# Sliding-window attention into an MLP: block 11's input transposed on TensorE and ScalarE instead of by DMA

## The chip, the cores and the metric

The kernel runs on one core of a Trainium2 chip. The metric is the device time of one execution in microseconds (us). A core has five engines that work at once, each in its own order: TensorE (PE: matmuls, with the weight loads PEld beside them), VectorE (DVE), ScalarE (ACT), GpSimd (POOL) and SyncE (SP). POOL and SP mostly issue DMA transfers here. Engines wait for each other with semaphores.

## The reference, cut to what matters

```python
# q, k, v: batch 8, heads 8, tokens 576, head size 64
scores = q @ k.T / 8 - slope[head] * |query - key|   # only 0 <= query - key < 128
x  = softmax(scores) @ v                             # heads side by side: (8, 576, 512)
xn = (x - mean(x)) / sqrt(var(x) + 1e-6) * g_ln
out = x + relu(xn @ w_ch1) @ w_ch2                   # 512 -> 2048 -> 512
```

## The kernel before, in words

**Blocks and groups.** The 8 x 576 tokens are cut into 36 blocks of 128: four pairs of batches, nine blocks each (eight full ones, and a ninth, `T`, that holds the 64 last tokens of both batches). Block number n is `p * 9 + blk`. `GROUPS = [2] * 4 + [4] * 7` puts blocks 0 to 7 into four groups of two and the rest into seven groups of four, so group 3 holds blocks 6 and 7, and group 4 holds blocks 8 to 11. `home[n]` gives the group of a block and its place in it.

**Attention of a block.** `attend` makes scores on TensorE (L407), ScalarE takes the exponential (L415), VectorE multiplies by the decay and mask (`masks`, L426). `values_at_once` multiplies by v on TensorE (L489); VectorE takes the reciprocal of the row sums (L497) and scales (L498), which gives x of the block. `centre` subtracts the row mean (L540), which gives `xc`, in fp16. `square` sums the squares of `xc` on ScalarE (L571); `inv_std` makes the inverse standard deviation of a whole group on VectorE (L585 to L603). That factor is multiplied in only at the end (L949, L831), so the MLP runs on `xc` itself.

**The transposed x.** The first layer needs x with its features on the partitions: tile `xT` of a group, four chunks of 128 features by up to 512 tokens. Blocks 0 to 7 (`BY_DMA = 8`) get it by `turn_x`: four TensorE transposes (matmuls with an identity, L560) into one PSUM tile `ps_tx`, and one copy to SBUF (L561) by VectorE or ScalarE. From block 8 on, `centre` issues one DMA transpose per block from SP (L550). SP's queue also carries the stores of the output (L970, L965) and, from block 18 on, the DMA transposes of q and k (`turn_natural`, L327); it is in order.

**The MLP of a group.** `mlp1` runs the first layer: for each of 16 chunks of 128 hidden units four matmuls with the whole group as the moving side (L718), and a ReLU by ScalarE (L734) or VectorE (L726). For groups of two, `mlp2` runs the second layer: for each block 16 matmuls (L748), then `finish` (L949) and `store`. Groups of four go through `mlp2_seven`, a scheme with seven products of half size instead of eight (L810, L831) with sums prepared on VectorE (L768).

**The order.** TensorE, ScalarE, VectorE and SP run in the order in which the program is written (`tc.manual_schedule`). The attention is a list of `steps`, four for each block from block 8 on; the MLP functions are generators that yield after every four first-layer matmuls or every two second-layer matmuls. `weave_at(units, *places)` runs the MLP unit by unit and, behind the units whose numbers it is given, the next step of the list. The second layer of group 3 carries all four steps of block 11, and the first layer of group 4 follows it:

```python
weave_at(mlp2(3), 0, 2, 3, 6, 9, 11, sums=4)
for g in range(4, len(GROUPS)):
    one, two = LEAD[g - 4]
    weave_at(mlp1(g, (6, 13) if one else ()), *one, seven=g)
```

The four steps of a block are: values, centring and the first scores of a later block; the second scores; the first masks and `square`; the second masks. Of block 11 they stand behind units 3, 6, 9 and 11 of the sixteen of `mlp2(3)`. The steps of block 12 begin behind unit 2 of `mlp1(4)`, that is, after twelve first-layer matmuls.

**PSUM.** One pool, `ps_mm`, of four banks serves the transposes (`ps_tx`, `ps_tr`), the accumulators of both layers (`ps_m1`, `ps_m2`, both shown as `ps_m` in the profile) and the seven products (`ps_s`); the scores have two tiles of their own, `ps_sc`.

**Loads.** POOL issues the loads of q, k and v in one list, six or seven blocks ahead; a load waits until its buffer is free.

Of the kernel before, what the change touches and what calls it, by code (L numbers as in the profile page):

```python
# [30 lines left out]
FIRST_GROUPS, FIRST = 2, 4  # L31

BY_DMA = SEEN = 8

# [36 lines left out]
def kernel(  # L73
# [10 lines left out]
    nc = tc.nc  # L84
# [148 lines left out]
    def by_dma(p, blk):  # L233
        return p * NSLOT + blk >= TURN_BY_DMA
# [10 lines left out]
    order = [(p, blk) for p in range(NPAIR) for blk in range(NSLOT)]  # L245
# [183 lines left out]
    def attends(p, blk):  # L429

        low, high, every = [0, 1], [2, 3], [0, 1, 2, 3]
        if blk == T:
            return [(p, T, [6, 7], m_ends, "probs", hps) for hps in (low, high)]
        if blk < 2:
            return [(p, blk, [blk], m_full[:, :, P:], "own", every)]
        return [(p, blk, [blk - 2, blk], m_full, "probs", hps) for hps in (low, high)]
# [5 lines left out]
    def tail_attend(p):  # L442
        return (p, T, [T], m_tail, "own", [0, 1, 2, 3])
# [66 lines left out]
    centred = {}  # L510

    def centre(p, blk):

        total = sums.pop((p, blk))
        mean = small.tile([P, 1], FP32, tag="mean", name="mean")
        if p * NSLOT + blk < BY_DMA:
            nc.vector.tensor_scalar(
                out=mean,
                in0=total[:, 0:1],
                scalar1=total[:, 1:2],  # L520
                scalar2=1.0 / DM,
                op0=ALU.add,
                op1=ALU.mult,
            )
        else:
            nc.vector.tensor_scalar(
                out=mean, in0=total[:, 0:1], scalar1=1.0 / DM, scalar2=None, op0=ALU.mult
            )
        xc = xc_pool.tile([P, DM], FP16, tag="xc", name="xc")
        if p == 0 and blk < FIRST:  # L530
            nc.vector.scalar_tensor_tensor(
                out=xc,
                in0=xs[p, blk],
                scalar=mean,
                in1=g_row,
                op0=ALU.subtract,
                op1=ALU.mult,
            )
        else:
            nc.vector.tensor_scalar(  # L540
                out=xc, in0=xs[p, blk], scalar1=mean, scalar2=None, op0=ALU.subtract
            )
        n = p * NSLOT + blk
        g, at = home[n]
        if at == 0:
            turned_x[g] = group_pool.tile([P, NKB, 4 * P], FP16, tag="xT", name="xT")
        if n < BY_DMA or g >= SEVEN:
            centred[p, blk] = xc
        if n >= BY_DMA:
            nc.sync.dma_start_transpose(  # L550
                out=turned_x[g][:, :, at * P : (at + 1) * P], in_=xc
            )

    def turn_x(g, at, p, blk, copy):

        xT = turned_x[g]
        xc = centred.pop((p, blk))
        ps = ps_mm.tile([P, NKB, P], FP16, tag="mm", name="ps_tx")
        for kb in range(NKB):
            nc.tensor.transpose(ps[:, kb, :], xc[:, kb * P : (kb + 1) * P], iden)  # L560
        copy(out=xT[:, :, at * P : (at + 1) * P], in_=ps)  # L561
# [47 lines left out]
    members, home = [], {}  # L609
    for g, size in enumerate(GROUPS):  # L610
        n = sum(GROUPS[:g])
# [5 lines left out]
    def turn_step(n, *how):  # L617
        p, blk = order[n]
        return [(turn, p, blk // 2) + how]
# [4 lines left out]
    def values_steps(n):  # L624
        p, blk = order[n]
        ahead = place[min(n + AHEAD + (n > TURN_BY_DMA - 10), count - 1)]
        return [
            [(load_until, ahead), (masks, p, blk), (values, p, blk, 0)],
            [(values, p, blk, 1), (centre, p, blk)],
        ]  # L630

    def x_step(n, copy=nc.vector.tensor_copy):
        return [(turn_x,) + home[n] + order[n] + (copy,)] if n < BY_DMA else []

    def variance_of(n):

# [5 lines left out]
    def warm_step(n):  # L642
        return [[(warm, n)]]


    steps = warm_step(11) + [[(turn_first,)]] + warm_step(3)
    steps += [scores_step(0), scores_step(1) + masks_of(0) + masks_of(1)] + warm_step(6)
    steps += values_steps(0)
    steps += [turn_step(2, True, (nc.scalar.copy, nc.scalar.copy))]
    steps += values_steps(1) + warm_step(4)  # L650
    steps += [x_step(0, nc.scalar.copy)] + warm_step(2) + [scores_step(2)]
    steps += [masks_of(2, 1) + x_step(1) + scores_step(3), values_steps(2)[0]]
    steps += [masks_of(2)]
    first = len(steps)

    steps += [values_steps(2)[1] + masks_of(3)]
    steps += [x_step(2, nc.scalar.copy), *values_steps(3), x_step(3, nc.scalar.copy)]

    steps += [variance_of(0) + variance_of(1), variance_of(2) + variance_of(3)]
# [14 lines left out]
    for n in range(8, count):  # L674
        ahead = place[min(n + AHEAD + (n > TURN_BY_DMA - 10), count - 1)]
        todo = []
        if n + 1 < count and order[n + 1][1] == T:
            todo.append(tail_attend(order[n][0]))
        if n + 2 < count:
            todo += attends(*order[n + 2])  # L680
        step = [(load_until, ahead), (masks,) + order[n]]
        step += [(values_at_once,) + order[n], (centre,) + order[n]]
        step += [(attend, *args, 1) for args in todo[:1]]
        second = [(attend, *args, 1) for args in todo[1:]]
        if n + 3 < count and order[n + 3][1] % 2 == 0 and not by_dma(*order[n + 3]):
            second += turn_step(n + 3)
        third = [(masks, *args[:2], 1) for args in todo[:1]] + [(square, n)]
        for tag, m in (("q", n + 4), ("k", n + 5)):
            if m < count and order[m][1] % 2 == 0 and by_dma(*order[m]):
                p, blk = order[m]  # L690
                third.append((turn_natural, tag, p, blk // 2))
        steps += [step, second, third, [(masks, *args[:2], 1) for args in todo[1:]]]
    TWICE = [4, 6, 8, 9, 11, 13, 15, 15], [3, 7, 11, 15, 19, 23, 27, 27]
    LEAD = [([2, 4, 5, 6, 7, 8, 9, 10, 12, 13, 15, 15], TWICE[1])]
    LEAD += 4 * [TWICE] + [(TWICE[0], [7, 11, 15, 19]), ([], [])]
# [352 lines left out]
```

## Time and profile before

| | |
|---|---|
| time before, median of 3 runs | 316.02 us (313.88 to 316.44) |
| the profiled execution, its own time | 316.07 us |
| its span | 314.3 us |
| TensorE busy | 302.9 us, 96% |
| VectorE busy | 233.9 us, 74% |
| ScalarE busy | 184.4 us, 59% |
| POOL busy | 107.9 us, 34% |
| mean granted TensorE clock | 0.994 of full speed |
| first layer, L718 | 576 matmuls, 119.5 us |
| DMA transposes of x, L550 | 28, median 4.4 us from issue to landing |

The span runs from the first to the last instruction of the profiled execution; what the execution's own time has beyond it lies around it. Times in the profile's rows are microseconds from the start of the span. A row of a timeline gives start, duration, engine, line, operation, output and inputs, shapes and count; in square brackets stands the idle time of the engine just before, and what ended it. A matmul's duration includes its way through the array, so matmuls in a row overlap, and the distance of their starts is shorter than the duration of one. The granted clock is 1.00 at full speed. The chain is the work that ended last, followed back from the last instruction.

### The profile page before, as it was taken

Reading aid. Unit: us, or ns where it says so; the run is one execution under the profiler, and the core shown is the slowest. Engines: PE = TensorE matmul, PEld = TensorE weight load, DVE = VectorE, ACT = ScalarE, POOL = GpSimd, SP = SyncE. Lnnn points to the kernel's source line nnn. Section 1 sums busy time; section 2 is a strip of 40 time slices with the busy share of each in tenths; the row PEclk is TensorE's granted clock in tenths of the full one; section 3 lists DMA queues with packets and bytes.
Section 4 is the critical chain, followed back from the end, with each engine's and each line's share of the span. In section 5 each row is a group of like instructions: output and inputs, shape, how many; then the busy total and the mean of one; then the engine's idle time right before and its main releaser. Section 6 shows DMA issues by size and latency. Waiting matters only on the chain.

```text
span 314.3 us, 9387 instructions
## 1 busy us (share of the span) xinstructions
PE 302.9 (96%) x3886; PEld 200.8 (64%) x3886; DVE 233.9 (74%) x629; ACT 184.4 (59%) x330; POOL 107.9 (34%) x148
## 2 busy tenths in 40 slices
PE   8889999998988999999999999999999999999994
PEld 3468655856733568755864686468656865785583
DVE  2689887697993889767976887688769876964563
ACT  6588766767944983467357735753676268405600
POOL 8923758769341634725251645120000000000000
PEclk9999999999997999999999999999999999999999
DMA  9999999999992999999999999993562143025004
GB/s 105 176 206 198 189 146 173 199 146 151 131 117 53 95 105 125 138 197 106 134 126 166 101 141 138 165 135 59 114 108 50 37 94 79 17 19 134 0 19 117
DMA packets 140316, 36.99 MB, mean 118 GB/s; under 512 B 131185, under 2 KB 135921, under 8 KB 140274
## 3 DMA queue, kind: packets, MB, share of 16 engines
q0 software_dynamic: 98560, 18.36, 85.2%
q1 hardware_dynamic: 41234, 17.52, 32.9%
q8 instruction: 30, 0.49, 0.7%
q10 hardware_dynamic: 480, 0.52, 0.5%
q14 instruction: 12, 0.10, 0.1%
HBM read 36.90 MB, written 9.44 MB: 147 GB/s over the span
## 4 chain that ended last, share of the span: by engine, by line
PE 83%; DVE 6%; DMA 5%; ACT 2%; POOL 2%; issue 1%; POOLq 0%
PE ps_m L718 39%; PE ps_s L810 24%; PE ps_sc L407 5%; PE ps_m L748 5%; PE ps_q L889 4%; PE ps_sc L489 4%; DMA k<-in_k_dram 2%; DMA xT<-xc 2%; DMA out_dram<-o 1%; ACT probs L415 1%; PE ps_pv L460 1%; POOL q L204 1%; DVE w L768 1%; DVE k L314 1%; DVE st L565 1%
## 5 line engine op out<-in xcount | busy, mean ns | idle before, releaser
L718 PE MATMUL ps_m<-xT,w1g 128*128 128x512 f16 (+1 forms) x576 | 119.5, 359 | 2.7 <-DMA xT<-xc 2.4
L734 ACT ACTIVATE ht_all<-ps_m 128x512 f16<-128x512 f32 (+1 forms) x159 | 81.9, 519 | 42.8 <-PE ps_m L718 40.6
L718 PEld LDWEIGHTS <-w1g 128*128 128x128 f16 x576 | 54.3, 98 | 54.1 <-issue 5.9
L415 ACT ACTIVATE probs<-ps_sc 128x1024 f16<-128x1024 f32 x56 | 56.6, 1029 | 48.0 <-PE ps_sc L407 48.0
L239 POOL DMA_DIRECT2D vx<-in_v_dram x40 | 34.5, 867 | 33.4 <-PE ps_sc L489 24.8
L810 PE MATMUL ps_s<-w,s 128*128 128x256 f16 x384 | 43.8, 273 | 0.0
L810 PEld LDWEIGHTS <-s 128*128 128x128 f16 x384 | 36.7, 98 | 4.7
L426 DVE TENSOR_TENSOR probs<-probs,m 128x1024 f16<-128x1024 f16 x56 | 36.9, 683 | 1.7 <-ACT probs L415 1.7
L810 PE MATMUL ps_s<-w,ht_all 128*128 128x256 f16 x288 | 34.3, 273 | 0.0
L768 DVE TENSOR_TENSOR s<-ht_all 128x1024 f16<-128x1024 f16 (+2 forms) x35 | 20.4, 582 | 18.3 <-ACT ht_all L734 17.7
L228 POOL DMA_DIRECT2D q<-in_q_dram x32 | 21.9, 703 | 30.2 <-DMA q<-q 23.5
L748 PE MATMUL ps_m<-w,ht_all 128*128 128x512 f16 x128 | 31.0, 380 | 0.0
L810 PEld LDWEIGHTS <-ht_all 128*128 128x128 f16 x288 | 27.4, 98 | 5.0
L831 DVE SCALAR_TENSOR_TENSOR o<-ps_s,rstd,x 128x256 f32<-128x256 f32 x48 | 21.0, 479 | 11.1 <-PE ps_s L810 11.1
L407 PE MATMUL ps_sc<-q,k 64*64 64x128 f16 (+1 forms) x1088 | 24.0, 209 | 0.9 <-ACT probs L415 0.8
L407 PEld LDWEIGHTS <-k 64*64 64x64 f16 x1088 | 15.9, 106 | 12.8 <-issue 10.3
L571 ACT ACTIVATE junk<-xc 128x512 f16<-128x512 f16 x28 | 17.6, 627 | 4.9 <-DVE xc L540 4.8
L498 DVE SCALAR_TENSOR_TENSOR x<-ps_sc,rec 128x512 f16<-128x512 f32 x28 | 19.4, 692 | 1.0
L831 DVE SCALAR_TENSOR_TENSOR o<-ps_s,rstd,o 128x256 f32<-128x256 f32 x36 | 15.7, 479 | 4.5 <-PE ps_s L810 4.4
L748 PEld LDWEIGHTS <-ht_all 128*128 128x128 f16 x128 | 11.2, 98 | 11.2
L225 POOL DMA_DIRECT2D k<-in_k_dram x16 | 14.4, 916 | 10.9 <-DMA k<-k 10.9
L415 ACT ACTIVATE own<-ps_sc 128x1024 f16<-128x1024 f32 x12 | 12.1, 1032 | 9.2 <-PE ps_sc L407 9.2
(88 smaller groups left out, 343.4 us busy)
## 6 DMA issues: line engine op xcount, KB each, us to landing
out_dram<-o SPq DMA_DIRECT2D x66, 128.0 KB, 3.5
k<-in_k_dram POOLq DMA_DIRECT2D x32, 128.0 KB, 6.0
vx<-in_v_dram POOLq DMA_DIRECT2D x32, 128.0 KB, 6.6
w<-in_moe_w_ch_dram POOLq DMA_DIRECT2D x8, 512.0 KB, 10.5
q<-in_q_dram POOLq DMA_DIRECT2D x40, 64.0 KB, 4.2
q<-in_q_dram POOLq DMA_DIRECT2D x16, 128.0 KB, 7.2
k<-in_k_dram POOLq DMA_DIRECT2D x8, 64.0 KB, 4.8
vx<-in_v_dram POOLq DMA_DIRECT2D x8, 64.0 KB, 4.7
```

What stands on the lines that cost most here:

```text
L228: nc.gpsimd.dma_start(out=t[half, b], in_=tokens.rearrange("h (c r) d -> r c h d", r=2)[r],)
L239: nc.gpsimd.dma_start(out=vx[p0 : p0 + n, :, 0:D], in_=v[b, :, t0 : t0 + n, :].rearrange("h p d -> p h d"),)
L407: nc.tensor.matmul(in_halves(ps[cols, j, n, t, :])[:, r, queries], kt[rows, hp, cols], in_halves(qt[rows, b, hp])[:, r, queries], start=Tr ...
L415: nc.scalar.activation(out=dst.rearrange("p (n j) q -> p j n q", j=2), in_=ps.rearrange("p j n t q -> p j n (t q)"), func=AF.Exp, scale=in ...
L426: nc.vector.tensor_tensor(out=dst, in0=dst, in1=mask, op=ALU.mult)
L498: nc.vector.scalar_tensor_tensor(out=x.rearrange("p (h d) -> p h d", h=H), in0=ps[:, :, 0:D], scalar=1.0, in1=rec.unsqueeze(2).broadcast_t ...
L718: nc.tensor.matmul(ps[:, 0:cols], w[:, kb, fb * P : (fb + 1) * P], xT[:, kb, 0:cols], start=(kb == 0), stop=(kb == NKB - 1),)
L734: nc.scalar.activation(out=ht[:, fb, :], in_=ps[:, 0:cols], func=AF.Relu)
L748: nc.tensor.matmul(sums[at], ht[:, fb, at * P : (at + 1) * P], w2[:, fb, :], start=(fb == 0), stop=(fb == NFB - 1),)
L768: nc.vector.tensor_tensor(out=out, in0=a, in1=b, op=op)
L810: nc.tensor.matmul(ps[:, pair, :], lhs[:, fb, at : at + P], rhs[:, fb, :], start=(first and pair == 0 and fb == 0), stop=(fb == half - 1), ...
L831: nc.vector.scalar_tensor_tensor(out=outs[at][:, cols], in0=ps[:, pair], scalar=rstd[:, n : n + 1], in1=(xs[p, blk] if fresh else outs[at] ...
```

## The change

Block 11 is taken out of the DMA path: `centre` issues no DMA transpose for it, and `turn_x` does its four transposes on TensorE and the copy on ScalarE. These stand in block 11's fourth step, behind unit 11 of `mlp2(3)`. The second masks of the block's step list move from the fourth step to the third, and `square` of block 11 from the third to the fourth, behind the copy. `turn_x` no longer takes `xc` out of the dictionary, since `square` reads it afterwards. All other blocks are handled as before.

```diff
+IN_HASTE = 11
 ...
-        if n >= BY_DMA:
+        if n >= BY_DMA and n != IN_HASTE:
             nc.sync.dma_start_transpose(
                 out=turned_x[g][:, :, at * P : (at + 1) * P], in_=xc
             )
 ...
     def turn_x(g, at, p, blk, copy):
 
         xT = turned_x[g]
-        xc = centred.pop((p, blk))
+        xc = centred[p, blk]
 ...
     def x_step(n, copy=nc.vector.tensor_copy):
-        return [(turn_x,) + home[n] + order[n] + (copy,)] if n < BY_DMA else []
+        return [(turn_x,) + home[n] + order[n] + (copy,)] if n < BY_DMA or n == IN_HASTE else []
 ...
-        steps += [step, second, third, [(masks, *args[:2], 1) for args in todo[1:]]]
+        fourth = [(masks, *args[:2], 1) for args in todo[1:]]
+        if n == IN_HASTE:
+            third, fourth = third[:1] + fourth, x_step(n, nc.scalar.copy) + third[1:]
+        steps += [step, second, third, fourth]
```

In the built program, VectorE's and POOL's instructions are the same and in the same order as before. SP has one DMA transpose less. TensorE has four weight loads and four transposes more, behind the eighth of the sixteen second-layer matmuls of block 7. ScalarE has the copy more, ahead of `square` of block 11.

## The prediction

> **What bounds the kernel now.** I read the page first: shares, slices, chain.
>
> ```profile
> span 314.3 us, 9387 instructions
> PE 302.9 (96%) x3886; PEld 200.8 (64%) x3886; DVE 233.9 (74%) x629; ACT 184.4 (59%) x330; POOL 107.9 (34%) x148
> ...
> PEclk9999999999997999999999999999999999999999
> ...
> PE 83%; DVE 6%; DMA 5%; ACT 2%; POOL 2%; issue 1%; POOLq 0%
> ```
>
> TensorE is busy for 302.9 of 314.3 us and makes 83% of the chain, so an edit counts by what it does to TensorE's stream. One of the 40 slices shows a granted clock below 9: the thirteenth, 94.3 to 102.1 us. TensorE's own waits come next, with total, times and longest:
>
> ```profile
> PE ps_m L718 <- DMA xT<-xc: 2.4, 1, 2.4
> ...
> PE ps_sc L407 <- ACT probs L415: 0.8, 3, 0.5
> ```
>
> The longest is a single wait of 2.4 us: a first-layer matmul (L718) waits for an x transposed by DMA. The chain in order of time shows which:
>
> ```profile
> 88.74 0.06 DVE xc L540
> ...
> 89.44 5.77 DMA xT<-xc
> ...
> 95.45 4.44 PE ps_m L718 x12
> ```
>
> At 88.74 VectorE centres block 11, the last member of group 4; its transpose is issued at 89.44 and takes 5.77 us; only then can group 4's first layer begin. The windows around it give busy time (PE, PEld, DVE, ACT, POOL), then granted clock, DMA share and GB/s:
>
> ```profile
> 84.00:88.00 4.00, 4.00 (x124) 2.54 (x113) 3.97 (x9) 3.54 (x8) 3.21 (x5) 1.00 1.36 70
> 88.00:93.00 5.00, 5.00 (x38) 2.05 (x36) 4.93 (x10) 2.06 (x4) 2.16 (x3) 1.00 1.73 115
> 93.00:95.45 2.45, 0.04 (x1) 0.03 (x1) 2.17 (x11) 0.00 (x0) 0.00 (x0) 1.00 1.69 186
> 95.45:97.00 1.55, 1.55 (x5) 0.60 (x6) 0.04 (x1) 0.00 (x0) 0.00 (x0) 0.58 0.45 106
> 97.00:99.00 2.00, 2.00 (x6) 0.66 (x5) 0.00 (x0) 0.75 (x2) 0.00 (x0) 0.50 0.03 8
> 99.00:101.00 2.00, 2.00 (x38) 1.31 (x37) 0.55 (x2) 1.31 (x3) 0.34 (x1) 0.97 0.00 0
> ```
>
> After the stall the clock is 0.58, then 0.50, and is back at about 99 us. So the late transpose is paid twice: as idle time, and as slow matmuls.
>
> **The change, part by part.** *Removed: the wait.* TensorE's rows on both sides, and the same twelve matmuls a little later:
>
> ```profile
> 88.98 4.06 PE L748 MATMUL ps_m<-w,ht_all 128*128 128x512 f16 x18
> 95.45 4.44 PE L718 MATMUL ps_m<-xT,w1g 128*128 128x512 f16 x12 [2.42 <-DMA xT<-xc]
> 99.72 0.65 PE L489 MATMUL ps_sc<-vx,probs 128*128 128x65 f16 x16
> ...
> 103.30 2.96 PE L718 MATMUL ps_m<-xT,w1g 128*128 128x512 f16 x12
> 106.09 0.65 PE L489 MATMUL ps_sc<-vx,probs 128*128 128x65 f16 x16
> ```
>
> The idle time is 2.42 us; it goes if x is ready in time (below). Term: -2.42.
>
> *Removed: the slow clock.* Twelve equal matmuls take 4.44 us after the stall and 2.96 us at 103.30. Term: 2.96 - 4.44 = -1.48. Counted to the next group's start, it is (99.72 - 95.45) - (106.09 - 103.30) = 4.27 - 2.79 = 1.48, the same. Its bounds are 0, if the clock falls here for another reason, and 1.48. The Trainium skill (TensorE: Matmul & The Clock Gate, Part 1: The HAM clock gate) has the clock halve after an idle window of about 3.4 us, longer than this stall. By that rule the stall would not explain the fall and this term would be 0; the trace, with 0.58 straight after 2.42 us, speaks for the stall.
>
> *Added: four transposes on TensorE and a copy on ScalarE.* The kernel does the same for blocks 0 to 7:
>
> ```profile
> 26.77 0.38 PE ps_tx L560 x4
> L560 PE MATMUL ps_tx<-iden,xc x32: 219/219/230, 15.5 to 62.2; 128*128 128x128 f16 x32
> L561 ACT COPY xT<-ps_tx x3: 579/586/628, 16.4 to 27.2; 128x512 f16<-128x512 f16 x3
> ```
>
> In the chain four transposes take 0.38 us. Unpipelined they would be 4 x 0.219 = 0.88. I take 0.38, since the stream around them is as dense here; the bounds are 0.38 and 0.88. Term: +0.38. The Trainium skill (the same page, Part 4: PE-mode transpose) puts a transpose at about 275 ns in a kernel, 390 alone, and says that transposes do not count as busy for the gate. By its 275 ns the estimate would be 1.1 us and the sum 313.3. The row with 0.38 for four decides against that.
>
> *Is the input there?* For the time at which TensorE gets there, the group of the second layer (count, busy, mean ns):
>
> ```profile
> L748 PE MATMUL ps_m<-w,ht_all 128*128 128x512 f16 x128 | 31.0, 380 | 0.0
> ```
>
> In the built order the transposes stand after unit 11 of the second layer of group 3: behind ten of the 18 matmuls at 88.98, ahead of the last eight. The last of 18 lasts 0.38 us from its start, so a slot is (4.06 - 0.38) / 17 = 0.216 us. So TensorE reaches them at 88.98 + 10 x 0.216 = 91.1. Block 11's xc:
>
> ```profile
> 88.74 0.67 DVE L540 TENSOR_SCALAR xc<-x,mean 128x512 f16<-128x512 f16 x1
> ...
> 93.08 0.75 DVE L949 SCALAR_TENSOR_TENSOR o<-ps_m,rstd,x 128x512 f32<-128x512 f32 x1
> ...
> 95.32 0.17 DVE L603 SCALAR_TENSOR_TENSOR rstd<-hh,rstd 128x4 f32<-128x4 f32 x1
> 100.42 0.21 DVE L497 RECIPROCAL rec<-ps_sc 128x8 f32<-128x8 f32 x1 [4.93 <-PE ps_sc L489]
> ```
>
> It is done at 89.41, 1.7 us early. VectorE's order does not change.
>
> *Is the copy out of the way?* ScalarE's rows:
>
> ```profile
> 89.11 1.02 ACT L415 ACTIVATE probs<-ps_sc 128x1024 f16<-128x1024 f32 x1 [0.68 <-PE ps_sc L407]
> 90.03 0.62 ACT L571 ACTIVATE junk<-xc 128x512 f16<-128x512 f16 x1
> ...
> 97.14 0.60 ACT L734 ACTIVATE ht_all<-ps_m 128x512 f16<-128x512 f32 x1 [6.41 <-PE ps_m L718]
> ```
>
> The transposes end at 91.1 + 0.38 = 91.5, with up to 0.22 for the last to come through; the copy runs from 91.7 to 92.3. Group 4's first matmul is due after the eight remaining slots, at 91.5 + 8 x 0.216 = 93.2. So those eight hide the copy with 0.9 us to spare; with that cover gone it would cost 0.22 + 0.59 = 0.8. Behind the copy in ScalarE's queue stands block 11's square (L571), which moves from 90.03 to 92.3 and ends near 93.1. Its reader is the inverse deviation of group 4 on VectorE, behind the output sum that now starts at 93.5 and ends at 94.2. So it costs nothing, in ScalarE's gap of 6.41 us. PSUM: the new tile takes one of four shared banks; in the built order the next first-layer tiles wait for banks freed by then, and none of the first three for block 7's sum.
>
> *Removed from SP: one DMA transpose.* The store behind it waits for its own data anyway (SP, POOL, and the landings of xT):
>
> ```profile
> 84.35 1.19 SPq L550 DMA_TRANSPOSE xT<-xc  x1
> 89.44 1.19 SPq L550 DMA_TRANSPOSE xT<-xc  x1
> 90.72 1.18 SPq L970 DMA_DIRECT2D out_dram<-o  x2
> 100.66 0.88 POOL L239 DMA_DIRECT2D vx<-in_v_dram  x1 [10.49 <-PE ps_sc L489]
> DMA to landing us min/median/max: 2.8/5.4/6.0
> ```
>
> The store's sum L949 of block 6 ends at about 90.7, so SP gains nothing: 0. Group 4 still waits for three DMA transposes; the last of them, block 10's at 84.35, is in by 90.4 even with the longest landing of any x from 60 to 140 us (6.0).
>
> *What is late next.* TensorE reaches block 12's values about 3.5 us sooner, at 96.2. VectorE by then has the output sum and the inverse deviation behind it: that ended at 95.32 + 0.17 = 95.49, 1.7 after the sum (93.08 + 0.75 = 93.83), so 94.2 + 1.7 = 95.9 now, in time for the reciprocal (L497), due near 96.9 (0.7 behind the values, as before). POOL's next load waits for TensorE (10.49 us) and moves with it, into DMA engines that are nearly idle (share 0.03 at 97). TensorE's later stretches, and its only other late wait, both from 100 us on:
>
> ```profile
> PE ps_sc L407 <- ACT probs L415: 0.3, 2, 0.2
> ...
> 100.00:140.00 40.00, 39.64 (x572) 26.16 (x569) 31.44 (x81) 26.25 (x43) 20.13 (x26) 1.00 1.43 125
> 140.00:200.00 60.00, 60.00 (x699) 40.35 (x696) 47.83 (x126) 35.91 (x59) 25.07 (x33) 1.00 1.64 135
> 200.00:260.00 60.00, 60.00 (x697) 40.64 (x700) 47.03 (x122) 34.52 (x57) 2.27 (x3) 1.00 0.71 89
> ```
>
> It is full to 260 us, and its one wait there follows its own scores. I find nothing that keeps its absolute time, so the gain should last to the end: 0 given back.
>
> *Sum*, against the profiled execution's 316.07 us (span 314.3 and 1.77 around it): 316.07 - 2.42 - 1.48 + 0.38 = 312.55. That execution is 0.05 above the median of 316.02. I say 312.5.
>
> **The rivals.**
>
> *The clock falls anyway* (chance 0.09): the gate closes on something else near 95 us, or closes at another place once the pace changes. For it: one shown run took 313.88, 2.2 below the profiled one, so something of that size varies between runs. Against it: the clock is 1.00 before the stall and 0.58 right after. Time: 316.07 - 2.42 + 0.38 = 314.03. The rule of the Trainium skill on the 3.4 us window (TensorE: Matmul & The Clock Gate, Part 1), weighed above, would give this same time.
>
> *The copy becomes the wait* (0.09): TensorE stands at group 4's first matmul until ScalarE has written xT. For it: ScalarE is in order and its exponentials of 1.02 us stand just ahead. Against it: 0.9 us of margin, and 0.62 us of ScalarE work (the square) leaves the queue's head. Cover gone entirely and unpipelined transposes: 312.55 + 0.8 + 0.5 = 313.9; half of that is 313.2.
>
> *The change doesn't take the wait away* (0.03): group 4 also needs the DMA transposes of blocks 8 to 10; if the DMA engines, not the late issue, set the date, TensorE waits on for them. Time: 316.07 + 0.38 = 316.45. Against it: 90.4 at the latest, as above.
>
> *TensorE takes over VectorE's lateness: slower* (0.05). Now the whole in-order stream stands at the transposes until xc is there, with eight second-layer matmuls behind them, which used to run meanwhile. VectorE is busy 3.97 of 4 and 4.93 of 5 us here, so nothing of a delay would be caught up. The price is the slip less 1.7, plus 1.48 if the clock halves again. With that, the break-even is 2.42 + 1.48 - 0.38 - 1.48 = 2.04 us of stall, a slip of 3.7 us. A slip of 5 gives a stall of 3.3, and 312.55 + 3.3 + 1.48 = 317.3. Against it: nothing is put ahead of xc on VectorE.
>
> **How the numbers follow.** The forecast has 0.74: 312.5, with its own range 312.2 to 313.1 (transposes at 0.88 above; below, a dead time of 95.45 - 88.98 - 18 x 0.216 = 2.6 us, if slots rather than ends are counted). The whole range, 311.3 to 314.4, takes in the first two rivals, and below a part of the 2.6 us spread of the runs shown (313.88 to 316.44), whose cause I can't see. About 1% is what a measurement of this kernel can tell; faster by more is below 312.9. That has most of the forecast's 0.74: 0.68 for faster. Same: the rest of it, both middle rivals and the third, 0.28. Slower by over 1%: 0.04 of the last rival's 0.05.
>
> **What would show it.** Right: no wait of L718 for DMA near 93; granted clock 1.00 throughout 93 to 101; four L560 transposes near 91 in about 0.4 us; the copy (L561) on ScalarE done before group 4's first matmul; twelve first-layer matmuls in about 2.9 us; block 12's values at about 96 instead of 99.72; later stages all earlier by the same 3.5 us. Wrong: a stall at the transposes or at the first L718; a slice with a lower clock elsewhere; or a later wait of TensorE above 0.5 us that is not there now, which would be the gain given back.

## The result, and the profile after

| | before | changed |
|---|---|---|
| median of 11 runs | 313.93 us (313.16 to 316.44) | 312.28 us (311.69 to 312.97) |
| profiled execution, its own time | 316.07 us | 312.28 us |
| span | 314.3 us | 310.5 us |
| its mean granted clock | 0.994 | 1.000 |

The ratio is 0.9931, with a 95% interval of 0.9906 to 0.9956: faster by 0.7%, not by the forecast 1.1%. (The ratio, here and below, is estimated from the runs of both kernels, without a run over 1.5% above the fastest of its kernel; the quotient of the two medians is 0.995.) The time of the changed kernel was forecast to 0.2 us (312.5), in part by luck, as the part on the prediction shows. What was not foreseen is the other side of the ratio: over 11 runs the kernel before is 2.1 us faster than the three runs shown first, and than the profiled one.

The page of the changed kernel: span, TensorE's share, and its granted clock in the 40 slices; then what is left of the waits of the first layer (L723 here, L718 before).

```profile
span 310.5 us, 9392 instructions
...
PE 301.1 (97%) x3890; PEld 200.3 (65%) x3890; DVE 234.2 (75%) x629; ACT 185.1 (60%) x331; POOL 108.1 (35%) x148
...
PEclk9999999999999999999999999999999999999999
```

```profile
PE ps_m L723 <- DMA w<-in_moe_w_ch_dram: 0.4, 1, 0.4
PE ps_m L723 <- ACT k L316: 0.3, 1, 0.3
```

The wait for `xT` is gone, and so is the slice with the low clock. The timeline around the place, three engines together:

```profile
89.13 0.67 DVE L542 TENSOR_SCALAR xc<-x,mean 128x512 f16<-128x512 f16 x1
...
89.37 2.33 PE L753 MATMUL ps_m<-w,ht_all 128*128 128x512 f16 x10
...
91.54 0.39 PE L562 MATMUL ps_tx<-iden,xc 128*128 128x128 f16 x4
...
91.76 1.89 PE L753 MATMUL ps_m<-w,ht_all 128*128 128x512 f16 x8
91.96 0.59 ACT L563 COPY xT<-ps_tx 128x512 f16<-128x512 f16 x1 [1.44 <-PE ps_tx L562]
...
92.98 0.19 ACT L573 ACTIVATION_READ_ACCUMULATOR junk<-xc 128x1 f32 x1
...
93.49 2.75 PE L723 MATMUL ps_m<-xT,w1g 128*128 128x512 f16 x12
...
95.94 0.16 DVE L605 SCALAR_TENSOR_TENSOR rstd<-hh,rstd 128x4 f32<-128x4 f32 x1
...
96.08 0.65 PE L491 MATMUL ps_sc<-vx,probs 128*128 128x65 f16 x16
...
96.77 0.21 DVE L499 RECIPROCAL rec<-ps_sc 128x8 f32<-128x8 f32 x1 [0.68 <-PE ps_sc L491]
```

xc is done at 89.80, the copy at 92.55, and the first layer, at 93.49, follows the second without a gap. The windows of the stall of before (the last three numbers are granted clock, DMA share, GB/s):

```profile
93.00:95.45 2.45, 2.45 (x14) 1.09 (x12) 2.05 (x8) 0.80 (x4) 0.00 (x0) 1.00 0.42 99
95.45:97.00 1.55, 1.55 (x37) 1.08 (x36) 0.75 (x5) 1.16 (x2) 0.00 (x0) 1.00 0.73 169
97.00:99.00 2.00, 2.00 (x31) 0.87 (x30) 1.21 (x4) 1.65 (x3) 0.88 (x1) 1.00 0.18 11
```

**A measure free of the start.** The first 20 us wait for loads and differ by up to 3 us between executions. So I compare *the stretch*: from the first of the 18 last second-layer matmuls of group 3 to block 12's first v matmul. Before it is 99.72 - 88.98 = 10.74 us, now 96.08 - 89.37 = 6.71: a gain of 4.03. What comes ahead of the stretch is 0.39 longer in this execution, and what follows (314.3 - 99.72 = 214.58, 310.5 - 96.08 = 214.42) is 0.16 shorter: 4.03 - 0.39 + 0.16 = 3.80 of span.

### The profile page after: what moved, and what is told of

Its sections match the earlier page's. It is cut to its first block, busy times and chain, and to the rows that moved or that the text cites. A ratio compares the mean times of both kernels' runs of the same rounds, so it can differ in the third digit from the quotient of the medians.

```text
span 310.5 us, 9392 instructions
## 1 busy us (share of the span) xinstructions
PE 301.1 (97%) x3890; PEld 200.3 (65%) x3890; DVE 234.2 (75%) x629; ACT 185.1 (60%) x331; POOL 108.1 (35%) x148
## 4 chain that ended last, share of the span: by engine, by line
PE 85%; DMA 6%; POOL 3%; DVE 3%; issue 1%; ACT 1%; SPq 0%; POOLq 0%
PE ps_m L723 38%; PE ps_s L815 24%; PE ps_m L753 7%; PE ps_sc L409 5%; DMA w<-in_moe_w_ch_dram 4%; PE ps_sc L491 4%; PE ps_q L894 4%; DMA out_dram<-o 1%; POOL vx L241 1%; POOL k L206 1%; POOL q L206 1%; POOL w L167 1%; ACT probs L417 1%; PE ps_pv L462 1%; DVE st L567 1%
## 5 line engine op out<-in xcount | busy, mean ns | idle before, releaser
L723 PE MATMUL ps_m<-xT,w1g 128*128 128x512 f16 (+1 forms) x576 | 117.8, 356 | 0.3 <-ACT k L316 0.3
L723 PEld LDWEIGHTS <-w1g 128*128 128x128 f16 x576 | 53.9, 98 | 50.2 <-issue 0.8
L409 PEld LDWEIGHTS <-k 64*64 64x64 f16 x1088 | 15.8, 107 | 12.6 <-issue 10.2
```

Source lines behind the costliest of these rows:

```text
L409: nc.tensor.matmul(in_halves(ps[cols, j, n, t, :])[:, r, queries], kt[rows, hp, cols], in_halves(qt[rows, b, hp])[:, r, queries], start=Tr ...
L723: nc.tensor.matmul(ps[:, 0:cols], w[:, kb, fb * P : (fb + 1) * P], xT[:, kb, 0:cols], start=(kb == 0), stop=(kb == NKB - 1),)
```

## The experiments

Each ratio is against runs of the kernel before on the same chip; their median was 313.95 to 314.55 us on the four chips used.

**1. Nine fillers in the stall.** The kernel before, and:

```diff
             one, two = LEAD[g - 4]
+            if g == 4:
+                warm(9)          # nine 128x512 matmuls on ones, read by nobody
```

> The kernel before, with block 11 still transposed by DMA, and nine 128x512 matmuls on ones ahead of group 4's first layer, which fill 9 x 0.216 = 1.9 us of the 2.4 us stall and feed nothing. Theory A (the stall costs 2.0 net in every execution, and 1.5 more in those executions in which the clock falls after it; the runs of before near 316 are those, the ones near 313.9 are not): group 4 still starts when the DMA lands, near 95.4; the clock is 1.00 in all executions, none is above 315, and the median stays at 313.7 to 314.3. Theory B (the clock falls after the stall in every execution, and the spread of before has another cause): 1.5 is saved in all, the median is 312.4, as with the change. Theory C (the clock falls near 95 us for a reason other than the idle time): the profile still shows a granted clock near 0.5 behind the fillers, and nothing is saved.

Measured: median 314.95, ratio 1.0032 (0.9997 to 1.0067).

```profile
91.50 4.06 PE L748 MATMUL ps_m<-w,ht_all 128*128 128x512 f16 x18
95.40 2.10 PE L276 MATMUL ps_warm<-ones 128*128 128x512 f16 x9
98.52 2.75 PE L718 MATMUL ps_m<-xT,w1g 128*128 128x512 f16 x12 [1.01 <-issue]
101.11 0.65 PE L489 MATMUL ps_sc<-vx,probs 128*128 128x65 f16 x16
```

Twelve matmuls in 2.75 instead of 4.44 us: with 1.01 us of idle time left, the clock does not fall here. That speaks against C. B falls by the median. But A's numbers missed too: the first layer starts 7.02 us into the stretch (6.47 before), and four of twelve executions were at 317.8 to 318.6, with a mean clock of 0.987 to 0.995. In the profiled one, of 317.85, the fall lies at the start, from about 15 to 18 us, mostly in the third slice (15.8 to 23.7 us):

```profile
PEclk9989999999999999999999999999999999999999
```

```profile
13.08 0.44 PE L294 MATMUL ps_sc<-iden,q 64*64 64x64 f16 x30 [0.69 <-DMA q<-in_q_dram]
```

The second row is TensorE's longest idle time between 8 us and that fall, 0.69 us, one of several short ones. So the clock can also fall without a long stall, and at another place. Experiment 7 repeats this with fewer fillers.

**2. The order alone.** The kernel before, and in block 11's steps:

```diff
+        fourth = [(masks, *args[:2], 1) for args in todo[1:]]
+        if n == 11:
+            third, fourth = third[:1] + fourth, third[1:]
```

> The kernel before with only the change's new order of block 11's steps (both masks in the third step, the square in the fourth), block 11 still by DMA. My theory gives the order no part in the gain: same as before within 0.2 us, the wait of L718 for the DMA transpose of 2 to 2.6 us still there. Rival (the gain comes from the masks or the square standing elsewhere): 312.3 to 313.

Measured: median 314.67 against 314.55, ratio 0.9988 (0.9957 to 1.0018).

```profile
90.13 4.06 PE L751 MATMUL ps_m<-w,ht_all 128*128 128x512 f16 x18
96.06 2.75 PE L721 MATMUL ps_m<-xT,w1g 128*128 128x512 f16 x12 [1.88 <-DMA xT<-xc]
98.65 0.65 PE L489 MATMUL ps_sc<-vx,probs 128*128 128x65 f16 x16
```

```profile
97.00:99.00 2.00, 2.00 (x21) 1.05 (x20) 0.00 (x0) 1.34 (x3) 0.00 (x0) 1.00 0.21 47
```

The order shows no part in the gain. This profile shows what the one of before did not: the same stall, here 1.88 us, *without* a fall of the clock. The stretch is 8.52.

**3. Block 10 instead of block 11.** The changed kernel with `IN_HASTE = 10`.

> The changed kernel's code applied to block 10 instead of 11: one DMA transpose less as well, four transposes and a copy more, but the last member of group 4 still comes by DMA. My theory (what counts is that the last member's DMA lands late): the stall stays at 2 to 2.6 us, the 0.4 us of transposes disappears in it, and the time is that of before, 313.7 to 314.4. Rival (one DMA transpose less in the queue is what helps, since it lets the others land sooner): the wait shrinks below 1 us and the time is 312.3 to 313.

Measured: median 316.51 against 314.55, ratio 1.0035 (1.0005 to 1.0064).

```profile
88.52 4.06 PE L753 MATMUL ps_m<-w,ht_all 128*128 128x512 f16 x18
94.71 4.45 PE L723 MATMUL ps_m<-xT,w1g 128*128 128x512 f16 x12 [2.13 <-DMA xT<-xc]
99.00 0.65 PE L491 MATMUL ps_sc<-vx,probs 128*128 128x65 f16 x16
```

```profile
95.00:97.00 2.00, 2.00 (x6) 0.73 (x5) 0.03 (x1) 0.44 (x1) 0.00 (x0) 0.50 0.35 83
```

The stall stays at 2.13: one transpose less in the queue does not bring the others sooner, so the gain is about the last member. The median came out worse than expected. The mean clock is 0.995 or less in 7 of 12 executions, against 9 of 35 of before. The clock is not the whole of it: the five others have a median of 315.8, those of before 314.2. Why both came out worse, these runs don't tell.

**4. No cover.** The changed kernel, and:

```diff
-            weave_at(mlp2(3), 0, 2, 3, 6, 9, 11, sums=4)
+            weave_at(mlp2(3), 0, 2, 3, 6, 9, 15, sums=4)
```

> The changed kernel with block 11's fourth step behind unit 15 of the second layer of group 3 instead of unit 11, so that no matmuls stand between the four transposes and group 4's first layer. My theory: TensorE waits for the transposes to come through (0.2) and for ScalarE's copy (0.6), 0.8 to 1.0 us in all, clock at 1.00, and the time is 313.1 to 313.3, against 312.3 with the cover. Rival (the copy is hidden anyway, or the wait makes the clock fall): 312.3, or 314.6.

Measured: median 312.98, ratio 0.9944 (0.9920 to 0.9969).

```profile
88.69 4.06 PE L753 MATMUL ps_m<-w,ht_all 128*128 128x512 f16 x18
92.59 0.39 PE L562 MATMUL ps_tx<-iden,xc 128*128 128x128 f16 x4
93.65 2.75 PE L723 MATMUL ps_m<-xT,w1g 128*128 128x512 f16 x12 [0.67 <-ACT xT L563]
96.23 0.65 PE L491 MATMUL ps_sc<-vx,probs 128*128 128x65 f16 x16
```

The median is 0.1 below the expected 313.1 to 313.3. The stretch is 7.54, 0.83 above the changed kernel's 6.71, the clock stays up: the eight matmuls behind the transposes hide 0.8 us, as the prediction priced them.

**5. The copy on VectorE.** The changed kernel with `x_step(n)` in place of `x_step(n, nc.scalar.copy)`.

> The changed kernel with VectorE instead of ScalarE copying the transposed block (0.42 us there against 0.59). It stands behind the masks on VectorE, which end at 92.86 in the profile of the changed kernel, so it would end near 93.3, where group 4's first matmul is due. My theory (VectorE is full here and ScalarE has a gap): TensorE waits 0.1 to 0.3 us for the copy, and VectorE's chain to block 12 comes 0.3 later; time within 0.4 us of the changed kernel, 312.3 to 312.8. Rival (the engine does not matter at all): no wait of L723 at all and the local stretch, from the 18 second-layer matmuls to block 12's values, stays at 6.7 us.

Measured: median 312.21, ratio 0.9954 (0.9930 to 0.9977).

```profile
92.69 0.41 DVE L563 COPY xT<-ps_tx 128x512 f16<-128x512 f16 x1
```

```profile
89.28 2.33 PE L753 MATMUL ps_m<-w,ht_all 128*128 128x512 f16 x10
...
93.40 2.75 PE L723 MATMUL ps_m<-xT,w1g 128*128 128x512 f16 x12
95.99 0.65 PE L491 MATMUL ps_sc<-vx,probs 128*128 128x65 f16 x16
```

No wait, and the stretch is 6.71: the rival held. The copy ends at 93.10, 0.3 us ahead of its reader. I had placed it 0.2 us too late.

**6. Block 12's values in the stall.** The kernel before, and:

```diff
-    LEAD = [([2, 4, 5, 6, 7, 8, 9, 10, 12, 13, 15, 15], TWICE[1])]
+    LEAD = [([-1, 4, 5, 6, 7, 8, 9, 10, 12, 13, 15, 15], TWICE[1])]
```

> The kernel before, block 11 by DMA, with block 12's first step (values, centring, first scores) ahead of group 4's first layer instead of behind its first twelve matmuls: useful work of 0.8 us in the stall. My theory (the stall is TensorE time that anything ready can fill, and a shorter stall keeps the clock): the wait for the DMA shrinks from about 2 to about 1.2 us, the granted clock stays at 1.00, and the median is 0.8 below the executions of before in which the clock holds: 313.1 to 313.6, none above 315. Rival (the work that is pulled forward is missed later): 314 or more, with a new wait of TensorE above 0.5 us.

Measured: median 315.54 against 313.95, ratio 1.0040 (1.0014 to 1.0067). Wrong, and not by the rival's mechanism. Chain, TensorE and windows:

```profile
89.12 7.46 DMA xT<-xc
```

```profile
96.83 6.16 PE L718 MATMUL ps_m<-xT,w1g 128*128 128x512 f16 x20 [3.32 <-DMA xT<-xc]
```

```profile
88.00:93.00 5.00, 5.00 (x52) 2.45 (x50) 4.92 (x11) 1.75 (x4) 1.85 (x3) 1.00 2.91 97
...
99.00:101.00 2.00, 2.00 (x6) 0.76 (x5) 0.00 (x0) 0.63 (x2) 0.00 (x0) 0.50 0.00 0
```

The transpose took 7.46 us instead of 5.77, and the wait grew although 0.8 us of work had been put into it. The DMA share beside it was 2.91, against 1.73 in that window before. What raised that share is not shown, but it pointed to the transpose's neighbours, hence experiments 9 and 10.

**7. Five fillers.** As 1, with `warm(5)`.

> As the nine fillers before, but five (1.1 of some 2 us). The nine fillers kept the clock at 1.00 behind the stall, but the stretch was 1 us longer than without, by a DMA landing 6.3 us or more after issue. If the fillers themselves cost time, five cost less: stretch from the 18 second-layer matmuls to block 12's values near 8.9. If that landing was chance, the stretch is what the landing gives, 8.3 to 9.0, clock 1.00, median 313.9 to 314.3 and none above 315.2. Rival (idle time does not decide on the clock): a third of the executions near 316 again, with a mean clock of 0.995.

Measured: median 313.65 against 313.95, ratio 0.9982 (0.9963 to 1.0002).

```profile
90.39 4.06 PE L748 MATMUL ps_m<-w,ht_all 128*128 128x512 f16 x18
94.29 1.24 PE L276 MATMUL ps_warm<-ones 128*128 128x512 f16 x5
96.04 2.75 PE L718 MATMUL ps_m<-xT,w1g 128*128 128x512 f16 x12 [0.51 <-issue]
98.62 0.65 PE L489 MATMUL ps_sc<-vx,probs 128*128 128x65 f16 x16
```

Eleven of twelve executions lie between 313.06 and 314.76 with a mean clock of at least 0.997; the twelfth, 315.10 at 0.992, has its fall at the start. The stretch is 8.23. With 0.51 us of idle time left the clock does not fall here, as in experiment 1. The executions with a clock above 0.995 have a median of 313.7, those of before on this chip 313.8: where the clock holds anyway, fillers save nothing. One low mean clock in 12, beside 5 in 35 of before on this chip, is too few to say how often they save the rest.

**8 and 11. The changed kernel again,** on two chips.

> The changed kernel again, on the same chip and beside the same runs of the kernel before as these three. The mean clock is above 0.996 in all executions and the median is 312.0 to 312.8, 1.5 to 2.0 below the executions of before whose clock holds and 3.4 to 4.0 below those whose clock falls (mean clock 0.996 or less). If what tells the two sets of before apart is not the clock at this place, the changed kernel shows two sets as well.

> The changed kernel on the same chip as the held loads, so that the two can be compared: median 312.0 to 312.8, stretch 6.7.

Measured: 312.28 and 312.23, ratios 0.9933 (0.9907 to 0.9958) and 0.9936 (0.9902 to 0.9970). The stretch of the second is 96.26 - 89.55 = 6.71, as expected. The expectation on the clock missed: of these 24 executions five have a mean clock of 0.995 or less, four of them in the first dozen. That dozen shows two sets, six at 311.3 to 311.7 and six at 312.8 to 313.6, which the expectation names as the sign that something else than the clock at this place parts the sets of before. None of the changed kernel's three profiles shows a fall, so where it lies in those five is open; the start is the likely place, since it falls there in the profiles of experiments 1, 7 and 9. Eight's profile has a wait that otherwise only experiment 1 shows, with 0.4 us:

```profile
140.57 0.37 PE L409 MATMUL ps_sc<-q,k 64*64 64x128 f16 x16 [1.13 <-DMA q<-q]
```

A later DMA transpose can be late too, now and then; it is not a price of the change, since the other two profiles of the changed kernel don't have it.

**9. The neighbours of the transpose left out.** The kernel before, and in `load_natural`:

```diff
         raw[tag, p, i] = t
+        if (p, i) == (2, 1):
+            nc.gpsimd.memset(t, 0.0)
+            return
```

> The kernel before, block 11 by DMA, but the loads of q and k of blocks 20 and 21 left out (GpSimd fills those tiles with zeros instead), six transfers that POOL issues between 84.8 and 90.2 and that are in flight beside block 11's transpose; the attention of these two blocks is computed on zeros. Nothing else is changed. Theory A (the transpose is late because it shares the DMA engines with these loads): it lands 2.5 to 4 us after issue instead of 5.2 to 7.5, TensorE's wait is below 0.6 us, the clock stays at 1.00, and the median is 312.0 to 312.6, as low as with the change. Theory B (a transpose of this size simply takes that long): landing above 5, wait about 2, median 313.7 to 314.3.

Measured: median 312.21 against 314.36, ratio 0.9918 (0.9888 to 0.9948).

```profile
91.07 4.06 PE L751 MATMUL ps_m<-w,ht_all 128*128 128x512 f16 x18
94.97 2.75 PE L721 MATMUL ps_m<-xT,w1g 128*128 128x512 f16 x12
97.56 0.65 PE L492 MATMUL ps_sc<-vx,probs 128*128 128x65 f16 x16
```

```profile
88.00:93.00 5.00, 5.00 (x67) 2.59 (x65) 4.89 (x12) 3.69 (x7) 1.36 (x2) 1.00 0.62 61
```

No wait, a DMA share of 0.62, a stretch of 6.49: theory A. No row shows the landing itself, but the first layer starts 3.8 us after the transpose's issue at 91.2. The stall was the loads' doing. A small part of it is an earlier issue: VectorE's subtraction for block 11 takes 0.35 us here and in experiment 10, 0.67 before, and the transpose is issued 0.3 us earlier in the stretch; why is not shown. This execution's start had a gap and a fall of its own:

```profile
14.54 0.44 PE L297 MATMUL ps_sc<-iden,k 64*64 64x64 f16 x30 [2.25 <-DMA k<-in_k_dram]
```

```profile
16.00:18.00 2.00, 2.00 (x20) 0.89 (x22) 1.40 (x4) 1.77 (x4) 1.02 (x2) 0.50 1.25 208
```

**10. The same loads held, not left out.** A complete kernel: before, without the `load_until` of blocks 10 and 11, which moves to block 11's third step, and:

```diff
         raw[tag, p, i] = t
+        if (p, i) == (2, 1):
+            g, at = home[11]
+            nc.gpsimd.tensor_copy(
+                out=t[:, :, 0, 0:1], in_=turned_x[g][:, 0:2, at * P : at * P + 1]
+            )
```

> A complete kernel: the kernel before, block 11 by DMA, where the same six loads of q and k of blocks 20 and 21 are not left out but held until block 11's transpose has landed (GpSimd first copies two elements of the landed tile into theirs, and the loads overwrite them). No instruction of TensorE, ScalarE or VectorE changes. My theory (the loads make the transpose late, and nothing needs them before 115): landing near 3 us, no wait of L718 above 0.3 us, clock 1.00, the stretch from the 18 second-layer matmuls to block 12's values 6.5 to 6.8, the median 312.0 to 312.5, level with the changed kernel or up to 0.3 below it, since TensorE has no transposes to do. Rival (the loads are missed later, since POOL is 5.5 us of work behind): a new wait of TensorE for a DMA of q or k above 0.5 us between 105 and 145, and 313 or more.

Measured: median 312.16, ratio 0.9947 (0.9916 to 0.9979); the changed kernel beside it 312.23.

```profile
89.51 4.06 PE L755 MATMUL ps_m<-w,ht_all 128*128 128x512 f16 x18
93.41 2.75 PE L725 MATMUL ps_m<-xT,w1g 128*128 128x512 f16 x12
96.00 0.65 PE L494 MATMUL ps_sc<-vx,probs 128*128 128x65 f16 x16
```

```profile
92.28 0.48 POOL L217 COPY q<-xT 128x2 f16<-128x2 f16 x1 [3.56 <-DMA xT<-xc]
```

POOL sees the landed tile at 92.28, 2.6 us after the transpose's issue at 89.66, and the stretch is 6.49. The DMA path is as fast as the changed one once its neighbours wait; the 0.22 us by which its stretch is shorter are below what the times can tell.

## Why the prediction was right, and where it was not

*The stall.* Right in its mechanism: no wait for `xT` is left. Its size was a little low: from the stretch's start to group 4's first layer it is 6.47 us before and 3.90 with the loads held, 2.57 less, not 2.42. *Input, copy, square, VectorE's chain.* The order of events and the margins were right: xc 1.5 us ahead of the transposes' weight loads at 91.33 and 1.7 ahead of the transposes (1.7 forecast), the copy 0.9 ahead of its reader (0.9). The dates fit within 0.2 us (square ended at 93.17 against 93.1, inverse deviation at 96.10 against 95.9, block 12's values at 96.08 against 96.2), but only because the stretch itself begins 0.39 us later in this execution; counted from its start, block 12's values come 0.5 us earlier than forecast (6.7 against 7.2). *The cover* was worth 0.83 (0.8). *Nothing given back:* the rest after block 12 takes 214.42 us against 214.58.

*The transposes* were mis-sized: +0.38 was the duration of the group, its way through the array included. In a dense stream the next matmul starts 0.22 us after the first transpose (91.54 to 91.76), and 6.71 - 6.49 = 0.22 between the changed kernel and the held loads says the same. *The slow clock* was mis-sized the other way: -1.48 by the profile, 4.44 - 2.75 = 1.69 in the twelve matmuls (1.68 by starts: 4.27 - 2.59). By starts the three terms add up to the stretch: 2.57 + 1.68 - 0.22 = 4.03, where the forecast had 3.52. That 312.5 came so close to 312.28 is in part luck: the 0.51 that the terms lack is nearly made up by the start, 0.39 longer in the changed kernel's profiled execution.

*What failed is the last line of the sum*: that the profiled execution stands for the median, being 0.05 above it. It carries both terms, and the second belongs to some executions only. Of 105 executions of the kernel before that ran beside the experiments, 21 have a mean clock of 0.995 or less, with a median of 315.8 us; the other 84 have 314.0. The clock's loss fits in size: half a percent of 314 us is 1.6. In how many of the 21 the fall lies at this stall is not shown: the profiles of experiments 1, 7 and 9 have such a mean clock by a fall at the start, and 5 of 35 executions of the changed kernel, which has no stall here, have it too. Four profiles with the stall show both kinds: 2.42 us (before), 2.13 and 3.32 with a fall, 1.88 without. In the larger set the change is worth the stall less the transposes: the changed kernel's executions with a clock above 0.995 have a median of 312.0, 2.0 below 314.0, and the sum without the clock term gives 2.42 - 0.38 = 2.04. So close a fit is in part luck: with the measured sizes it is 2.57 - 0.22 = 2.35, and the stall differs between executions (1.88 us in experiment 2). Where the clock falls at the stall, as in the two profiles, the change is worth 4.03 in the stretch. The run at 313.88, which stood among the three, was the sign of it; I read it as a rival's instead of asking which of the two terms it lacked. The chance of 0.68 on more than 1% rested on that line.

*The rivals.* "The clock falls anyway" did not happen at this place: of the four profiles with a stall of 1.88 us or more, three have a fall behind it; with fillers in it (1, 7), and in the changed kernel's three profiles, the clock is 1.00 here. Its second half, a fall elsewhere, is open for the five executions above. The Trainium skill's idle window of about 3.4 us (TensorE: Matmul & The Clock Gate, Part 1: The HAM clock gate) is longer than the stalls of 2.13 and 2.42 that halved the clock; the measurement decides. "The copy becomes the wait" needs the cover gone (4), and then costs what was said. "The wait isn't taken away" and "slower" did not happen.

*Not asked at all:* why the transpose took 5.77 us. I took the duration as given; it was the loads of blocks 20 and 21 (9, 10).

What stays open: why block 10 in block 11's place is slower, with more falls of the clock; in how many executions of before the fall lies at this stall; and what besides the length of an idle time makes the clock fall, since 1.88 us left it up (2), 2.13 did not (3), and at the start several short ones of at most 0.69 us came before a fall (1, 7).

## What to carry to other kernels

Before an operation is moved off a slow DMA, look at what shares the DMA engines with it: starting six loads 8 us later took the wait away, brought no new wait of TensorE in its profile, and was worth as much as replacing the transfer. A sum made on one profiled execution holds for the kernel only as far as that execution's chance events (a granted clock below 1.00) are common to all; take such a term with the share of runs that show it. Where the start differs from run to run, compare stretches between two fixed instructions, not spans.

## What was not expected of the hardware

A DMA transpose of 128x512 fp16 from SBUF to SBUF landed 2.6 us after issue with the six loads held (10), and took 5.2 to 7.5 (2, 6) beside seven loads of 64 to 128 KB. Idle times of 2.13 (3) and 2.25 us (9) of TensorE were followed by a granted clock of 0.50; 1.88 (2), 1.01 (1) and 0.67 (4) were not. In experiments 1 and 7 it also fell to 0.50 at the start, behind several idle times of at most 0.69 us.
